# Adding the last two parts of a sum in SBUF instead of the last one

## The chip, the core and the metric

The kernel runs on one core of one Trainium2 chip. The metric is the device time of one execution, in microseconds (us). Before the change three runs took 773.85, 774.66 and 778.57 us, a median of 774.66 us.

## The reference

Attention in which a query sees only the keys of its own hash bucket, then two feed-forward layers, all in fp32. Cut to what matters here:

```
x = attention(q, k, v)                       # 2 x 8 heads, 768 tokens, 64 wide -> 1536 x 512
h = x @ w_in;  x = (h - tanh(h)) @ w_out     # first layer, hidden width 2048
g = x @ w_gate                               # second layer, hidden width 1536
out = (silu(g) * (x @ w_val)) @ w_out2       # 1536 x 512, fp32
```

The change lies in the last product, `... @ w_out2`.

## The kernel before

**Tiling.** The second layer goes over its hidden width in `NP2` = 6 parts of 256 columns, `i` = 0 to 5. Each part is computed for two halves of the tokens (`sb` = 0, 1, 768 tokens each) and each half for two blocks of 384 tokens (`t` = 0, 1). So there are four output blocks, called 0/0, 0/1, 1/0 and 1/1 here (`sb`/`t`), each 384 x 512. In each part a block has three output groups, `m` = 0 to 2, of 128 rows each: six matmuls (128 x 512, line 1099) into one PSUM bank. The products with `w_gate` and `w_val` (line 1045) come before the output groups of their part and are mixed with those of the part before, so that TensorE always has work.

**Where the sum over the parts is kept.** It lies in the output in HBM. Parts 0 to 4 copy each group out of PSUM into a stage in SBUF (line 1128, on ScalarE or VectorE). When the three groups of a block are there, one DMA of 768 KB carries them out: a plain store for part 0 (line 1143), and for parts 1 to 4 an accumulating DMA that GpSimd issues (line 1145), which adds the stage to the output. The stages are a ring of four, one for each block, in the tiles `acc_2601` (`sb` = 0) and `acc_2602` (`sb` = 1). Part 5 goes the other way: SyncE loads the block's sum from the output into its stage (line 1120), VectorE adds each group to it from PSUM (line 1123), and SyncE stores each group's 128 rows (line 1124). A load waits until the accumulating DMA of its block has landed, since both touch the same bytes of the output.

**PSUM.** An output group takes the next of four banks (`t`, `t`, `x`, `h`) and gives it back when its copy or its add has run.

**The order of the work.** Every operation of the program has a number, and `ORDER` lists for each engine the numbers in the order in which the engine runs them. Each engine is a queue: an instruction that waits holds up all behind it. SyncE runs the loads of the weights (line 461), of the sums and the last stores in one such queue, and GpSimd runs its arithmetic and the accumulating DMAs in another.

The last twelve output groups on TensorE are those of part 5, in the order 0/0, 0/1, 1/0, 1/1, three groups each.

Of the kernel before, what the change touches and what calls it, by code (L numbers as in the profile page):

```python
# [18 lines left out]
NB, NH, S, D = 2, 8, 768, 64  # L19
# [8 lines left out]
NP1, NP2 = F1 // 256, F2 // 256  # L28
# [18 lines left out]
def chunk_keys():  # L47
# [5 lines left out]
    for i in range(NP2):  # L53
# [51 lines left out]
    """,  # L105
    DVE="""
# [49 lines left out]
    """,  # L156
    ACT="""
# [40 lines left out]
    """,  # L198
    POOL="""
# [17 lines left out]
    """,  # L217
    SP="""
# [11 lines left out]
    """,  # L230
).items()}

# [1 line left out]
class Plan:  # L234
# [15 lines left out]
    def op(self, eng, fn, r=(), w=(), due=0.0, lat=None, late=False, after=0.0, alt=None, port=()):  # L250
        n = len(self.ops)
        deps = set()
        for k in r:
            deps.update(self.writers.get(k, ()))
        for k in w:
            deps.update(self.writers.get(k, ()))
            deps.update(self.readers.get(k, ()))
        for k in r:
            self.readers.setdefault(k, []).append(n)
        for k in w:  # L260
            if k in r:
                self.writers.setdefault(k, []).append(n)
            else:
                self.writers[k] = [n]
                self.readers[k] = []
        deps.discard(n)
        self.banks[n] = {k[:2] for k in (*r, *w) if k[0] == "s"}
        eng = {e: t * (1 if e == "PE" or not self.n_first else self.SAFE) for e, t in eng.items()}
        self.ops.append((eng, fn, deps, due, self.LAT if lat is None else lat, late, after,
                         ALT if alt is None else alt, port, self.PE_WAIT if "PE" in eng else 0.0))  # L270
# [100 lines left out]
def lsh_attention_moe_kernel(ctx: ExitStack, tc: tile.TileContext, qT, kT, vP, proj, cst, wts, out):  # L371
# [3 lines left out]
    op = plan.op  # L375
# [576 lines left out]
    stages = {}  # L952
# [124 lines left out]
    def out_group(layer, i, sb, j):  # L1077
# [6 lines left out]
        t, m = divmod(j, n)  # L1084
# [5 lines left out]
        def mm(e):  # L1090
# [12 lines left out]
           due=d, lat=0.25)  # L1103
        e = clock[0]
        aks = [("acc", sb, n * t + c) for c in range(n)]
        if layer == 1 and i in (0, NP1 - 1):
# [4 lines left out]
            else:  # L1111
                op({"DVE": dve(TB)}, lambda g: g.tensor_tensor(
                    out=acc_at(sb, j), in0=ps(), in1=acc_at(sb, j), op=ALU.add,
                ), r=[k, ("acc", sb, j)], w=[("acc", sb, j)], due=e, late=True)
        elif layer == 2 and i == NP2 - 1:
            if m == 0:
                parts = [stage(layer, c) for c in range(n)]
                stages["last"] = [(at_, key) for at_, key, _ in parts]
                o = out[sb * S + t * TB:sb * S + t * TB + TB, :].rearrange("(j p) c -> p j c", p=128)
                op({"SP": 0.5}, lambda g, at_=parts[0][0]: g.dma_start(out=at_(3).rearrange("p (j c) -> p j c", j=3), in_=o),  # L1120
                   r=[("o", sb, t)], w=[key for _, key, _ in parts] + [k for _, _, f in parts for k in f], due=e - 25, lat=4.0)
            at_, key = stages["last"][m]
            op({"DVE": dve(DM)}, lambda g: g.tensor_tensor(out=at_(), in0=ps(), in1=at_(), op=ALU.add), r=[k, key], w=[key], due=e)
            op({"SP": 0.5}, lambda g: g.dma_start(out=out[sb * S + j * 128:sb * S + j * 128 + 128, :], in_=at_()), r=[key], w=[], due=e)
        else:
            at_, key, first = stage(layer, m)
            op({"ACT": act(size), "DVE": dve(size)}, lambda g, at_=at_:
# [171 lines left out]
```

## Time and profile before

| what | value |
|---|---|
| median of 3 runs | 774.66 us (773.85 to 778.57) |
| the profiled execution | 775.52 us, its span 773.2 us |
| TensorE busy | 757.5 us, 98% of the span |
| VectorE busy | 602.1 us, 78% |
| ScalarE busy | 456.2 us, 59% |
| GpSimd busy | 359.8 us, 47% |

The span is what the trace covers; the execution's own time has 2.3 us around it. TensorE is the engine that is nearly always busy, so time can be saved only where it stands idle or runs at a lower clock, and lost wherever it is made to wait. [...]

### The profile page before, as it was taken

How to read it: one execution, taken by the hardware profiler on the slowest of the kernel's cores; microseconds unless marked ns; L12 is line 12 of the kernel's file. 1: busy time of each engine (PE TensorE's matmuls, PEld its weight loads, DVE VectorE, ACT ScalarE, POOL GpSimd, SP SyncE). 2: the span in 40 equal slices, each digit the busy share in tenths (PEclk: the TensorE clock that was granted, in tenths of full speed). 3: DMA queues.
4: the chain of work that ended last, by engine and by line, in shares of the span. 5: the costliest groups of instructions: out<-in, count | busy, mean ns of one | idle time of the engine just before them, and what ended most of it. 6: DMA issues, size and time to landing. Idle time of an engine off the chain costs nothing.

```text
span 773.2 us, 12380 instructions
## 1 busy us (share of the span) xinstructions
PE 757.5 (98%) x4342; PEld 666.8 (86%) x4342; DVE 602.1 (78%) x1075; ACT 456.2 (59%) x964; POOL 359.8 (47%) x387
## 2 busy tenths in 40 slices
PE   7999999999999999999999999999999999999996
PEld 4677677677767999999999999999999998999995
DVE  6878777888998678888677889998887768788373
ACT  5887788879876646555455456665554445545320
POOL 4755666966884743223124353734324544323120
PEclk9999999999999999999999999999999999999998
DMA  5754466356323016787585764323547476486486
GB/s 140 200 143 110 118 179 146 82 136 173 114 83 109 28 37 176 166 190 196 115 198 114 202 136 106 84 96 109 182 119 156 117 163 137 111 150 91 73 177 231
DMA packets 38733, 104.23 MB, mean 135 GB/s; under 512 B 4720, under 2 KB 10096, under 8 KB 38672
## 3 DMA queue, kind: packets, MB, share of 16 engines
q1 hardware_dynamic: 28288, 71.06, 29.9%
q0 software_dynamic: 9920, 31.59, 23.8%
q10 hardware_dynamic: 464, 0.80, 0.4%
q8 instruction: 34, 0.56, 0.3%
q14 instruction: 27, 0.22, 0.1%
HBM read 49.17 MB, written 18.87 MB: 88 GB/s over the span
## 4 chain that ended last, share of the span: by engine, by line
PE 87%; ACT 3%; DMA 3%; DVE 3%; POOL 2%; issue 1%; SPq 1%; ACTq 0%; DVEq 0%; POOLq 0%
PE bs L1045 31%; PE t L1099 16%; PE h L1099 7%; PE x L889 7%; PE s L836 7%; PE t L866 6%; PE x L1099 5%; PE x L1045 3%; ACT ct L848 2%; PE t L1045 2%; DVE m L846 1%; DMA acc<-out 1%; PE h L1045 1%; SPq L746 1%; POOL ct L855 1%
## 5 line engine op out<-in xcount | busy, mean ns | idle before, releaser
L1045 PE MATMUL bs<-x,wi 128*128 128x384 f32 x1200 | 231.4, 335 | 1.0 <-DVE ct L1028 1.0
L1045 PEld LDWEIGHTS bs<-x,wi 128*128 128x128 f32 x1200 | 210.6, 188 | 6.2 <-DVE ct L1028 1.7
L855 POOL TENSOR_SCALAR ct<-ct,r 128x768 f32<-128x768 f32 x96 | 94.2, 986 | 36.2 <-DVE r L854 23.9
L846 DVE TENSOR_REDUCE m<-s 128x1 f32<-128x768 f32 x96 | 91.0, 953 | 20.9 <-PE s L836 18.7
L848 ACT ACTIVATE ct<-s,m 128x768 f32<-128x768 f32 x96 | 86.5, 902 | 18.9 <-DVE m L846 8.3
L1025 ACT ACTIVATE ct<-bs 128x384 f32<-128x384 f32 x120 | 57.2, 490 | 67.6 <-PE bs L1045 63.2
L836 PE MATMUL s<-op 128*128 128x384 f32 x384 | 91.5, 362 | 2.7 <-ACT ct L848 2.3
L866 PE MATMUL t<-csb,ct 128*128 128x128 f32 x576 | 82.6, 275 | 2.1 <-ACT pt L872 1.0
L866 PEld LDWEIGHTS t<-csb,ct 128*128 128x128 f32 x576 | 66.8, 140 | 18.7 <-issue 5.6
L836 PEld LDWEIGHTS s<-op 128*128 128x128 f32 x384 | 63.8, 189 | 17.4 <-ACT ct L848 8.5
L872 ACT ACTIVATE pt<-t 128x384 f32<-128x384 f32 x135 | 62.2, 489 | 24.3 <-PE t L866 23.3
L1099 PE MATMUL t<-op,wo 128*128 128x384 f32 x384 | 75.7, 335 | 0.0
L889 PE MATMUL x<-pt,v 128*64 128x384 f32 x384 | 69.0, 494 | 0.0
L1099 PEld LDWEIGHTS t<-op,wo 128*128 128x128 f32 x384 | 67.2, 188 | 0.6 <-DVE ct L1128 0.3
L1099 PE MATMUL t<-wo,op 128*128 128x512 f32 x264 | 67.7, 393 | 0.0
L477 POOL TENSOR_TENSOR wi<-fs,wi 128x512 fp32r<-128x512 f32 (+1 forms) x29 | 45.5, 1569 | 38.9 <-ACT wi L475 38.1
L1136 POOL DMA_DIRECT2D acc<-ct x24 | 21.0, 888 | 78.5 <-ACT ct L1128 32.2
L1099 PEld LDWEIGHTS t<-wo,op 128*128 128x128 f32 x264 | 48.9, 188 | 8.3 <-DVE acc L1128 0.3
L889 PEld LDWEIGHTS x<-pt,v 128*64 128x64 f32 x384 | 24.7, 136 | 28.6 <-issue 28.0
L475 ACT ACTIVATE wi<-fs 128x512 fp32r<-128x512 f32 (+1 forms) x60 | 41.9, 701 | 12.2 <-DVE fs L495 3.8
L1145 POOL DMA_DIRECT2D out<-acc x16 | 20.8, 1300 | 57.5 <-ACT op L967 16.8
L1045 PE MATMUL bs<-op,wi 128*128 128x384 f32 x240 | 47.3, 334 | 0.0
(171 smaller groups left out, 1412.5 us busy)
## 6 DMA issues: line engine op xcount, KB each, us to landing
raw<-in_w SPq DMA_DIRECT2D x68, 512.0 KB, 3.5
acc<-ct POOLq DMA_DIRECT2D x24, 768.0 KB, 6.1
out<-acc POOLq DMA_DIRECT2D x16, 768.0 KB, 7.5
op<-raw SPq DMA_DIRECT2D x42, 192.0 KB, 3.2
op<-f SPq DMA_DIRECT2D x56, 96.0 KB, 3.3
v<-in_v SPq DMA_DIRECT2D x8, 384.0 KB, 4.2
out<-acc SPq DMA_DIRECT2D x4, 768.0 KB, 4.6
acc<-out SPq DMA_DIRECT2D x4, 768.0 KB, 5.8
```

What stands on the lines that cost most here:

```text
L475: op({"ACT": act(n)}, lambda e: e.activation(out=hi, in_=src, func=ACTF.Copy), r=rk, w=[wk + (0,)], due=due, late=late)
L477: op({"POOL": pool(n), "DVE": dve(n)}, lambda e: e.tensor_tensor(out=lo, in0=src, in1=hi.bitcast(F32), op=ALU.subtract), r=rk + [wk + (0,) ...
L836: g.matmul(out=s[:, kh, 0:TB], lhsT=(b, a)[first][:, q0], rhs=ks[kh][0 if first else 1], start=first, stop=not first,)
L846: op({"DVE": 0.87}, lambda g: g.tensor_reduce(out=m, in_=sv, axis=AX.XY, op=ALU.max, negate=True), r=[sk + (0,), sk + (1,)], w=[mk])
L848: op({"ACT": 0.9}, lambda g: g.activation(out=p.rearrange("p (a b) -> p a b", a=2), in_=sv, func=ACTF.Exp, bias=m, accum_out=sm), r=[sk + ...
L855: op({"POOL": 0.91}, lambda g: g.tensor_scalar(out=p, in0=p, scalar1=r, scalar2=1.0, op0=ALU.mult, op1=ALU.mult), r=[pk, rk], w=[pk])
L866: g.transpose(out=t_t[z][:, kt * 128:(kt + 1) * 128], in_=p[:, z * TB + kt * 128:z * TB + (kt + 1) * 128], identity=ident)
L872: g.activation(out=dst, in_=src, func=ACTF.Copy) if g is nc.scalar else g.tensor_copy(dst, src),
L889: g.matmul(out=x[r, :], lhsT=v[:, kt, r], rhs=pt_t[ptks[e][1]][:, kt, :], start=(kt == 0), stop=(kt == NKT - 1), tile_position=(0, 64 * e),)
L1025: op({"ACT": act(TB)}, lambda e: e.activation(out=dst, in_=bank(), func=ACTF.Copy), r=[bk], w=dk, due=due)
L1045: e.matmul(out=bank(), lhsT=w[:, wpart, wi * 256 + k * 128:wi * 256 + k * 128 + 128], rhs=x_at(sb, xn, xpart, k), start=first and m == 0, ...
L1099: e.matmul(out=ps(), lhsT=lhs, rhs=rhs, start=c == 0, stop=c == 5)
```

## The change

Part 4 now goes the way of part 5: at its first group the block's sum over parts 0 to 3 is loaded into the stage, and the groups of part 4 and then of part 5 are added there by VectorE. Only after part 5 are the rows stored. So the four loads stand one part earlier, the four accumulating DMAs of part 4 are gone, and twelve copies out of PSUM have become adds. The number of matmuls, of loads and of stores is the same. The lists of `ORDER` are written anew for the second layer, from its part 1 on; here two of the lines of SyncE's list stand for them.

```
@@ SyncE's list
-        3005 3077 3081 3153 3159 3167 3171 3243 3247 3319 3325 3356 3332 3334 3350 3358 3342 3376 3366 3361 3364
+        3005 3077 3081 3153 3159 3168 3172 3244 3248 3319 3166 3325 3214 3242 3288 3333 3349 3356 3341 3359 3362
...
@@ out_group
-        elif layer == 2 and i == NP2 - 1:
-            if m == 0:
+        elif layer == 2 and i >= NP2 - 2:
+
+            if m == 0 and i == NP2 - 2:
                 parts = [stage(layer, c) for c in range(n)]
-                stages["last"] = [(at_, key) for at_, key, _ in parts]
+                stages["last", sb, t] = [(at_, key) for at_, key, _ in parts]
...
-            at_, key = stages["last"][m]
+            at_, key = stages["last", sb, t][m]
             op({"DVE": dve(DM)}, lambda g: g.tensor_tensor(out=at_(), in0=ps(), in1=at_(), op=ALU.add), r=[k, key], w=[key], due=e)
-            op({"SP": 0.5}, lambda g: g.dma_start(out=out[sb * S + j * 128:sb * S + j * 128 + 128, :], in_=at_()), r=[key], w=[], due=e)
+            if i == NP2 - 1:
+                op({"SP": 0.5}, lambda g: g.dma_start(out=out[sb * S + j * 128:sb * S + j * 128 + 128, :], in_=at_()), r=[key], w=[], due=e)
```

In the rows of the order, `acc_2601` holds the stages of `sb` = 0 and `acc_2602` those of `sb` = 1; `out_0` is the output in HBM; a row without a count is one instruction. The changed file's list is one line shorter, so lines up to about 1110 have a number lower by one, and those behind the change one that is higher by one.

The end of SyncE's queue before: weights (line 461), loads of the sum (line 1120), stores (line 1124).

```order
L461 DMA raw_67<-in_w 128x512 x15
L1120 DMA acc_2601<-out_0 128x3x512 x2
L1124 DMA out_0<-acc_2601 128x512 x4
L1120 DMA acc_2602<-out_0 128x3x512 x2
L1124 DMA out_0<-acc_2601 128x512 x2
L1124 DMA out_0<-acc_2602 128x512 x6
```

The same place now (weights line 460, loads line 1120, stores line 1125):

```order
L460 DMA raw_67<-in_w 128x512 x12
L1120 DMA acc_2601<-out_0 128x3x512
L460 DMA raw_67<-in_w 128x512
L1120 DMA acc_2601<-out_0 128x3x512
L1120 DMA acc_2602<-out_0 128x3x512 x2
L1125 DMA out_0<-acc_2601 128x512 x6
L1125 DMA out_0<-acc_2602 128x512 x6
```

The two loads of `sb` = 1 stood behind four stores; now all four loads stand ahead of the first store, and one weight load has a load of the sum ahead of it.

The end of GpSimd's queue before: the accumulating DMAs (line 1145), the splits of weights (lines 477, 514) and of activations (line 962).

```order
L1145 DMA out_0<-acc_2601 128x3x512
L962 TENSOR_TENSOR op_86<-ct_90,op_86 128x384
L1145 DMA out_0<-acc_2602 128x3x512
...
L1145 DMA out_0<-acc_2602 128x3x512
L477 TENSOR_TENSOR wi_63<-fs_71,wi_63 128x768
L1145 DMA out_0<-acc_2602 128x3x512
L514 TENSOR_TENSOR wo_82<-f_75,wo_82 128x512
L1145 DMA out_0<-acc_2601 128x3x512
...
L1145 DMA out_0<-acc_2602 128x3x512 x2
```

And now (accumulating DMAs line 1146, splits lines 476, 513, 961):

```order
L1146 DMA out_0<-acc_2602 128x3x512
L513 TENSOR_TENSOR wo_80<-f_75,wo_80 128x512
...
L1146 DMA out_0<-acc_2601 128x3x512
L961 TENSOR_TENSOR op_86<-ct_90,op_86 128x384
L1146 DMA out_0<-acc_2602 128x3x512
...
L1146 DMA out_0<-acc_2602 128x3x512
L476 TENSOR_TENSOR wi_63<-fs_71,wi_63 128x768
L1146 DMA out_0<-acc_2602 128x3x512
L513 TENSOR_TENSOR wo_82<-f_75,wo_82 128x512
```

Of the last nine accumulating DMAs before, the last four (part 4) are gone. The five ahead of them keep their order: 0/0 of part 3, 1/1 of part 2, then 0/1, 1/0 and 1/1 of part 3. The one ahead of these five, 1/0 of part 2, had seven instructions between itself and them and has four now.

VectorE's queue before, near the end of part 4: copies (line 1128) among the arithmetic of part 5's activations.

```order
L1128 COPY acc_2602<-h_103 128x512
L962 TENSOR_TENSOR ct_90<-bs00_2406,ct_90 128x384
L1128 COPY acc_2602<-t_107 128x512
L1128 COPY acc_2602<-t_108 128x512
L962 TENSOR_TENSOR bs11_2396<-bs11_2396,ct_90 128x384
```

And now:

```order
L1123 TENSOR_TENSOR acc_2602<-h_103,acc_2602 128x512
L961 TENSOR_TENSOR ct_90<-bs00_2406,ct_90 128x384
L1123 TENSOR_TENSOR acc_2602<-t_107,acc_2602 128x512
L1123 TENSOR_TENSOR acc_2602<-t_108,acc_2602 128x512
L961 TENSOR_TENSOR bs11_2396<-bs11_2396,ct_90 128x384
```

The adds stand where copies stood. Over the whole program VectorE has 12 adds more (24 instead of 12), 2 copies fewer, and 6 fewer small instructions of the preparation, which are now GpSimd's; ScalarE has 10 copies fewer.

## Rows read from the trace of the kernel before

**Rows 1.** The page's busy time: us, share of the span, instructions.

```profile
PE 757.5 (98%) x4342; PEld 666.8 (86%) x4342; DVE 602.1 (78%) x1075; ACT 456.2 (59%) x964; POOL 359.8 (47%) x387
```

**Rows 2.** Waits of TensorE from 500 us on: total us, times, longest.

```profile
PE x L1099 <- DVE acc L1123: 2.7, 1, 2.7
PE bs L1045 <- DVE ct L1028: 1.0, 1, 1.0
```

**Rows 3.** The chain that ended last, its end: start us, us, what.

```profile
756.42 7.46 DMA acc<-out
...
763.97 0.70 DVE acc L1123
...
764.72 2.63 PE x L1099 x6
767.34 2.00 PE h L1099 x6
...
769.37 0.69 DVE acc L1123
```

**Rows 4.** The end by window: busy us by engine, granted clock, DMA share, GB/s.

```profile
762.00:765.00 3.00, 0.35 (x2) 0.29 (x2) 1.03 (x2) 0.00 (x0) 0.00 (x0) 1.00 0.76 294
765.00:767.00 2.00, 2.00 (x6) 1.58 (x6) 1.45 (x3) 0.00 (x0) 0.00 (x0) 0.52 0.76 281
767.00:769.50 2.50, 2.33 (x7) 1.46 (x6) 0.82 (x2) 0.00 (x0) 0.00 (x0) 0.70 0.75 280
```

**Rows 5.** TensorE's timeline: start us, us, line, what.

```profile
698.96 1.55 PE L1099 MATMUL t<-wo,op 128*128 128x512 f32 x6
...
710.66 1.55 PE L1099 MATMUL t<-wo,op 128*128 128x512 f32 x6
712.05 1.21 PE L1045 MATMUL bs<-op,wi 128*128 128x384 f32 x6
...
759.18 2.88 PE L1099 MATMUL t<-wo,op 128*128 128x512 f32 x12
```

**Rows 6.** What SyncE's queue waited for from 690 us on.

```profile
SPq L1120 <- DMA out<-acc: 49.2, 2, 38.2
```

**Rows 7.** SyncE's timeline: start us, us, line, what.

```profile
755.86 0.97 SPq L1120 DMA_DIRECT2D acc<-out  x2
```

**Rows 8.** DMA issues: queue, count, KB each, median us to landing.

```profile
out<-acc POOLq DMA_DIRECT2D x16, 768.0 KB, 7.5
...
acc<-out SPq DMA_DIRECT2D x4, 768.0 KB, 5.8
out<-acc SPq DMA_DIRECT2D x12, 256.0 KB, 2.2
```

**Rows 9.** GpSimd's timeline, part 3's accumulating DMAs: start us, us, idle before.

```profile
671.23 1.27 POOL L1145 DMA_DIRECT2D out<-acc  x1
...
688.50 1.29 POOL L1145 DMA_DIRECT2D out<-acc  x1 [7.36 <-ACT ct L1025]
...
696.80 1.30 POOL L1145 DMA_DIRECT2D out<-acc  x1 [5.96 <-ACT op L967]
...
704.29 1.30 POOL L1145 DMA_DIRECT2D out<-acc  x1 [4.30 <-DVE bs L1028]
```

**Rows 10.** Copies and adds out of PSUM: ns min/median/max, first and last start.

```profile
L1128 ACT ACTIVATE acc<-t x5: 599/599/600, 700.5 to 728.2; 128x512 f32<-128x512 f32 x5
L1128 DVE COPY acc<-t x3: 681/681/691, 716.8 to 739.8; 128x512 f32<-128x512 f32 x3
...
L1123 DVE TENSOR_TENSOR acc<-t,acc x6: 679/691/692, 746.6 to 765.8; 128x512 f32<-128x512 f32 x6
```

**Rows 11.** Part 4's stretch by window: busy us of PE, PEld, DVE, ACT, POOL.

```profile
680.00:700.00 20.00, 20.00 (x106) 18.51 (x105) 17.84 (x29) 10.95 (x22) 6.66 (x6) 1.00 0.76 135
700.00:720.00 20.00, 20.00 (x105) 18.33 (x104) 14.77 (x23) 8.33 (x17) 3.92 (x3) 1.00 0.71 113
720.00:740.00 20.00, 20.00 (x104) 18.38 (x103) 6.53 (x13) 7.10 (x15) 4.00 (x4) 1.00 0.48 103
```

75 rows, old and new, of tables (ACT, DVE, PE, POOL) are left out of this document.

## The prediction

> **What bounds the kernel now.** The page's busy times come first: TensorE is busy 757.5 us of a span of 773.2 us, and no other engine comes near it [rows 1]. With the same matmuls before and after, time can come only from TensorE's waits and from a clock below the full one. So the next view is TensorE's waits. From 500 us on, which holds all that the change touches, there are two: 1.0 us somewhere in the second layer, and 2.7 us for a VectorE add of line 1123 [rows 2]. The chain of waits tells where the second comes from. A load of the sum lands 7.46 us after its issue; the add behind it runs at 763.97; only then is a bank free for the group that starts at 764.72 [rows 3]. The last two groups then take 2.63 and 2.00 us, although a group takes 1.39 us elsewhere: the one at 710.66 gives way to the next work at 712.05 [rows 5]. [...]
>
> Why the load is late stands in SyncE's queue. The loads wait for the accumulating DMAs of part 4, 49.2 us in all [rows 6], and the second pair, for `sb` = 1, stands behind four stores (the order) and is issued from 755.86 on [rows 7], when TensorE needs the sums within a few microseconds.
>
> **The tail, which the change takes away.** In the changed order all four loads stand ahead of the first store and belong to part 4, so no group of part 5 waits for a DMA. Without the wait the last two groups follow the twelve matmuls that start at 759.18, which are two groups: 759.18 + 2 x 1.39 = 761.96, not 764.72. That is 2.76 us. At full clock the two take 2.78 us, not 2.63 + 2.00 = 4.63: 1.85 us more. Together **4.61 us**. What is late next? A group's bank is needed again three groups after the group ends, 3 x 1.39 = 4.17 us, and its add takes 0.69 us [rows 10], so the adds keep more than 3 us of room and the end stays one add and one store (2.2 us to landing [rows 8]) behind the last group, as now.
>
> **The loads, moved one part earlier.** They now wait for part 3's accumulating DMAs. In the trace those are issued at 671.23 (0/0), 688.50 (0/1), 696.80 (1/0) and 704.29 us (1/1) [rows 9]. The tightest of the pairs that I work out is 0/1: issued at 688.50, landed 7.5 us later [rows 8], at 696.0; a load as slow as the slowest seen, 7.46 us, ends at 703.5. TensorE is through with the first group of 0/1 at 712.05 [rows 5], and no add can run before. Room: 8.5 us. For 0/0 it is 671.23 + 7.5 + 7.46 = 686.2 against 698.96 + 1.39 = 700.35, 14.2 us. On SyncE one weight load now stands behind the first load and so behind an accumulating DMA that landed at 678.7; no row shows when TensorE would miss that weight, so I bound it by the same room and take nothing.
>
> GpSimd's queue decides those issue times. Two accumulating DMAs there stand 7.49 us apart, 696.80 and 704.29 [rows 9], which is one landing: the second seems to wait for the first. In the new order 1/0 of part 2 stands closer ahead of the five, so the chain may be pushed back, at worst by one landing of 7.5 us. That still fits into 8.5. Cost nothing; the cover is this room, and beyond it VectorE's queue would stand.
>
> **Copies into adds.** An add takes 0.691 us, a copy 0.681 on VectorE and 0.599 on ScalarE [rows 10]. Twelve adds more and two copies fewer on VectorE are 12 x 0.691 - 2 x 0.681 = 6.9 us; six small instructions leave it, so 6.9 is the upper end. It lies beside TensorE as long as VectorE has room: in part 4's stretch it is busy 17.84, 14.77 and 6.53 us of 20 [rows 11], so 2.2, 5.2 and 13.5 us are free. At least five copies there were ScalarE's [rows 10], 3.5 us more for VectorE, spread over 40 us. I take nothing; the other end is 6.9 us of waiting. ScalarE loses ten copies, 6.0 us, hidden as they were. GpSimd loses four issues of 1.3 us and the standing behind them, and gains some arithmetic: nothing on the path, since TensorE never waits for it here [rows 2]. Its four transfers of 768 KB go too; the matmuls wait for no transfer before the tail.
>
> **The lists anew.** The other wait, 1.0 us [rows 2], lies in the rewritten stretch. It may go, or a like one may come: between -1.0 and +1.0, I take 0.
>
> **Sum.** -4.61 us, all else 0. On the profiled execution: 775.52 - 4.6 = 770.9 us, a span of 768.6. The median of the three runs is 0.86 us below the profiled one: 774.66 - 4.6 = **770.1 us**. That is 0.6%, less than the 1% that a measurement here can tell from no change.
>
> **Rivals.**
>
> *The clock falls all the same.* Then only the idle time comes back: 774.66 - 2.76 = 771.9. For it: nothing shows that the two slow groups were slow for the gap alone. Against it: the clock is 1.00 in every part 4 window, where TensorE is always busy [rows 11], and is low only right behind the gap [rows 4]. [...] Here no row shows a low clock without a gap before it, so I give this 9%.
>
> *VectorE becomes the bound (slower).* The place is part 4: VectorE at 17.84 of 20 us before the stretch gets copies that were ScalarE's. If it falls behind, the banks come free late and TensorE stops. If all 6.9 us became waiting and the clock then cost 1.85 us as it did in the tail, 8.75 - 4.61 = 4.1 us is lost: 778.8. It decides from 2.8 us of waiting on, where 2.8 + 1.85 is the gain. For it: the first window's 89%. Against it: 21 us are free over the three windows, three times the addition. 7%.
>
> *A load of part 4 comes late.* The add at the head of VectorE's queue holds all its other work. It starts to count when a chain is over 8.5 us later than in the trace. Two landings more ahead of it, 15 us, leave 6.5 us of standing; the banks cover some 3.4 of it, so 3.1 + 1.85 us are lost against 4.61 won: 775.0. [...] 5%.
>
> **Chances and range.** The forecast has 77%, the rivals 9, 7 and 5%, and 2% is left for what none of them names. The forecast's own range is 770.1 less 1.0 (the other wait gone) and less 0.8 (the median against the lowest run, 773.85), and the same upward: 768.3 to 771.9. It takes in the clock rival just about. To leave out no more than 2 in 10 I reach partly into the slower cases: 768.3 to 773.6. Faster by over 1% (under 766.9) would take 7.8 us, more than the waits and the clock hold: 3%. Slower by over 1% (over 782.4) needs both slower cases at their worst: 4%. Within 1%: 93%.
>
> **What would show it.** In the profile after: no wait of TensorE for line 1123; the granted clock 1.00 up to its last group; the last six matmuls of 128 x 512 in about 1.4 us; four loads landed before 725 us, all ahead of the first store; twelve accumulating DMAs; TensorE's waits from 500 us on at 1 to 2 us in all. Wrong would be a wait of TensorE or VectorE between 680 and 745 us, on a load or on an add of part 4, or two slow groups at the end without a gap before them.

## The result, and the profile after

The changed kernel took 783.83 us (median of ten runs, 778.47 to 786.00), the kernel before in the same comparison 774.86 us (772.90 to 778.57). The ratio worked out from the runs is 1.0096, with a 95% interval of 1.0077 to 1.0115 (the two medians alone give 1.0116). So it is slower, by about 1%, where the forecast was 770.1 us and 0.6% faster. The profiled execution of the changed kernel is one of its quicker ones: 779.19 us, span 777.4, against 775.52 and 773.2 before. The traces below explain the 4.2 us between these two spans.

The page's busy time answers to [rows 1]: us, share of the span, instructions.

```profile
PE 757.4 (97%) x4342; PEld 667.9 (86%) x4342; DVE 601.2 (77%) x1079; ACT 451.0 (58%) x954; POOL 359.2 (46%) x389
```

TensorE is as busy as before. The time is in its waits. From 500 us on (total us, times, longest; answers to [rows 2]):

```profile
PE bs L1044 <- ACT ct L1024: 2.6, 1, 2.6
PE x L1044 <- DVE op L961: 2.1, 1, 2.1
PE bs L1044 <- DVE ct L1027: 2.1, 2, 1.4
```

TensorE's timeline says where they are (start us, us, line, what; in brackets the wait before):

```profile
608.47 3.28 PE L1044 MATMUL bs<-x,wi 128*128 128x384 f32 x12 [2.57 <-ACT ct L1024]
642.28 2.38 PE L1044 MATMUL bs<-x,wi 128*128 128x384 f32 x12 [0.70 <-DVE ct L1027]
669.77 1.31 PE L1044 MATMUL x<-x,wi 128*128 128x384 f32 x6 [2.14 <-DVE op L961]
693.87 2.35 PE L1044 MATMUL bs<-x,wi 128*128 128x384 f32 x12 [1.43 <-DVE ct L1027]
```

The wait for an add of line 1123 is gone, and four waits, 6.84 us together, stand where two, 1.02 and 2.65 us, stood. None is for a load of a sum. They are called the first to the fourth here; the second, 0.70 us, is for the same kind of instruction as the 1.02 us before, and the other three are new. The first and the third are also followed by a lower clock. The windows behind the first (busy us of PE, PEld, DVE, ACT, POOL, granted clock as a share of full speed, DMA share, GB/s):

```profile
609.00:610.00 1.00, 1.00 (x7) 1.00 (x6) 0.86 (x2) 1.00 (x3) 0.61 (x1) 0.80 0.72 295
610.00:611.00 1.00, 1.00 (x5) 1.00 (x4) 0.54 (x2) 0.73 (x2) 0.68 (x1) 0.50 0.00 0
...
612.00:613.00 1.00, 1.00 (x4) 0.81 (x3) 0.97 (x3) 0.73 (x2) 0.00 (x0) 0.50 0.00 0
```

What the clock withholds is the sum of (1 - clock) over the time: 0.2 + 3 x 0.5 = 1.7 us here, and the same again from 671 to 675 us (granted clock 0.52, 0.50, 0.50 and 0.77). At the end there is nothing of it. The end of the chain of waits answers to [rows 3]:

```profile
767.66 2.72 PE t L1098 x12
770.38 1.36 PE x L1098 x6
771.74 1.37 PE h L1098 x6
```

The groups follow each other without a gap and take 1.36 us, and the window there shows the full clock (answers to [rows 4]):

```profile
770.00:773.00 3.00, 3.00 (x14) 2.25 (x12) 1.38 (x2) 0.00 (x0) 0.00 (x0) 1.00 0.46 175
```

The account: waits 6.84 - 3.67 = +3.2 us, lower clock 2 x 1.7 - 1.7 = +1.7 us (before: 2 x 0.48 + 2.5 x 0.30 in [rows 4]), together +4.9 against +4.2 in the spans, 0.7 us too much. Most of that lies at the start: the same twelve matmuls (`x<-pt,v`) start at 86.10 us in the profile before and at 85.15 in this one, 0.95 us earlier.

**The first wait.** It goes back to SyncE, in part 0. In the kernel before, the last plain store of part 0, block 1/1, was issued at 573.31 us. Now it stands behind two more weight loads, and a weight load waits until VectorE has freed its buffer, here up to 14.8 us (`SPq L460 <- DVE fs L468`). SyncE's timeline:

```profile
560.81 0.43 SPq L1144 DMA_DIRECT2D out<-acc  x1
567.80 25.75 SPq L460 DMA_DIRECT2D raw<-in_w  x4
593.64 1.09 SPq L1144 DMA_DIRECT2D out<-acc  x1
```

The chain of waits continues from there:

```profile
593.64 8.10 DMA out<-acc
...
601.76 0.04 DVE acc L1129
...
604.32 2.11 DVE ct L961
...
608.03 0.39 ACT ct L1024
...
608.47 3.28 PE bs L1044 x12
```

The store reads its stage until 601.74, and the copy of the next part into that stage stands at the head of VectorE's queue until then, 2.79 us; ScalarE's copy waits 2.35 us. All of VectorE's work behind it is late. On top of that, one of its instructions on this chain (`ct<-ct`) now runs beside a split of weights on GpSimd and takes 2.19 us, where it takes 0.56 as a rule:

```profile
603.62 2.40 POOL L476 TENSOR_TENSOR wi<-fs,wi 128x768 fp32r<-128x768 f32 x1 [3.65 <-ACT wi L474]
604.24 2.19 DVE L961 TENSOR_TENSOR ct<-ct 128x384 f32<-128x384 f32 x1
```

So TensorE's wait comes from the late store and from a stretched instruction together; the experiment with the stores early shows how the two hang together.

**The third wait.** Here one instruction of VectorE takes 4.29 us. VectorE and GpSimd, start us, us, idle in brackets:

```profile
663.41 1.29 POOL L1146 DMA_DIRECT2D out<-acc  x1
...
664.24 1.79 POOL L513 TENSOR_TENSOR wo<-f,wo 128x512 fp32r<-128x512 f32 x1
664.50 4.29 DVE L465 SCALAR_TENSOR_TENSOR fs<-raw,fs 128x512 uint32<-128x512 uint32 x1
665.49 1.51 POOL L961 TENSOR_TENSOR ct<-ct 128x384 f32<-128x384 f32 x1
666.47 1.76 POOL L476 TENSOR_TENSOR wi<-fs,wi 128x512 fp32r<-128x512 f32 x1
...
669.18 0.54 DVE L961 TENSOR_TENSOR op<-x,op 128x384 fp32r<-128x384 f32 x1
```

The same instruction (ns min/median/max) takes 684 ns as a rule:

```profile
L465 DVE SCALAR_TENSOR_TENSOR fs<-raw,fs x40: 675/684/4291, 185.0 to 692.1; 128x512 uint32<-128x512 uint32 x40
```

It lasts until three splits on GpSimd, one behind the other, have run. Behind it in the queue is `op<-x,op`, for which TensorE waits 2.14 us. The accumulating DMA ahead of the splits is that of block 1/0 of part 2, at 649.36 us before and at 663.41 us now.

`raw` and `fs` are both in SBUF, and the 4.29 us end 0.56 us behind the third split, about the 0.68 us that the instruction takes alone: it looks as if it had stood until the splits were through and then run. What makes it stand is not shown, and the order of the starts does not settle it. Here VectorE's instruction starts 0.26 us behind the first split; at 704.49 us in the kernel before, and at 678.41 us in an experiment below, it starts over 0.6 us ahead of the split and is held all the same (2.97 and 2.72 us). GpSimd's times in a trace are rough, so this stays open.

**The fourth wait** has a cause of the same kind, at one remove:

```profile
683.28 1.51 POOL L961 TENSOR_TENSOR ct<-ct 128x384 f32<-128x384 f32 x1
683.37 1.71 DVE L462 TENSOR_SCALAR fs<-raw 128x512 uint32<-128x512 uint32 x1
...
687.25 0.33 SPq L460 DMA_DIRECT2D raw<-in_w  x1
687.75 0.38 SPq L1120 DMA_DIRECT2D acc<-out  x1
...
691.72 0.43 DVE L462 TENSOR_SCALAR f<-raw 128x512 uint32<-128x512 uint32 x1 [2.57 <-DMA raw<-in_w]
```

The instruction at 683.37 takes 1.71 us, where the like one at 688.73 takes 0.42. VectorE frees the weights' buffer late, the next weight load is issued late, and VectorE then waits for it. A load of the sum was issued 0.5 us behind that weight load, which made it a suspect as well.

### The profile page after: what moved, and what is told of

Read it like the earlier page. It is cut to its first block, busy times and chain, and to the rows that moved or that the text cites. A ratio compares the mean times of both kernels' runs of the same rounds, so it can differ in the third digit from the quotient of the medians.

```text
span 777.4 us, 12377 instructions
## 1 busy us (share of the span) xinstructions
PE 757.4 (97%) x4342; PEld 667.9 (86%) x4342; DVE 601.2 (77%) x1079; ACT 451.0 (58%) x954; POOL 359.2 (46%) x389
## 4 chain that ended last, share of the span: by engine, by line
PE 83%; DVE 6%; DMA 4%; ACT 2%; POOL 2%; issue 1%; SPq 0%; DVEq 0%; ACTq 0%; POOLq 0%
PE bs L1044 28%; PE t L1098 15%; PE x L888 8%; PE s L835 7%; PE h L1098 7%; PE t L865 6%; PE x L1098 5%; PE x L1044 2%; PE t L1044 2%; DMA raw<-in_w 1%; DVE m L845 1%; POOL ct L854 1%; ACT ct L847 1%; DMA out<-acc 1%; PE h L1044 1%
## 5 line engine op out<-in xcount | busy, mean ns | idle before, releaser
L961 POOL TENSOR_TENSOR ct<-ct 128x384 f32<-128x384 f32 x23 | 25.6, 1112 | 54.2 <-ACT ct L980 36.1
L961 POOL TENSOR_TENSOR op<-ct,op 128x384 fp32r<-128x384 f32 x31 | 34.7, 1153 | 32.4 <-ACT op L966 23.1
```

What stands on the lines that cost most here:

```text
L961: op({"DVE": dve(TB), "POOL": pool(TB)} if port else {"DVE": dve(TB) + 0.01}, lambda e: e.tensor_tensor(out=now(dst), in0=now(a), in1=b, o ...
```

## The experiments

The theory: the sum itself, changed as the diff says, gains what the forecast says, and the new lists lose more than that, by the late stores on SyncE and by GpSimd's splits beside VectorE. The rivals: the sum costs the time (its loads or its adds), or the clock does by itself. Numbers in the edits are operations: 2540 and 2624 are the stores of part 0 of blocks 0/1 and 1/1, 2949 is the accumulating DMA of 663.41, 3170 the instruction of 4.29 us, 2977 the one TensorE waits for, 3166 the first load of a sum, 3325 the last weight load. In the table "after" is the changed kernel; most rows are ten or twelve runs, the last one seven, and the old sum in the new lists and the load behind alone four. Each ratio is to runs of the kernel before made alongside (medians 775.13 to 775.73 us).

| kernel | median us | lowest to highest | ratio to before [95%] |
|---|---|---|---|
| changed sum, lists of before | 772.90 | 770.93 to 774.92 | 0.9962 [0.9938, 0.9986] |
| old sum, new lists | 786.53 | 784.99 to 788.65 | 1.0130 [1.0087, 1.0174] |
| after, stores early | 775.13 | 773.23 to 781.14 | 1.0007 [0.9976, 1.0037] |
| after, split behind | 779.31 | 774.87 to 783.11 | 1.0046 [1.0021, 1.0071] |
| after, both | 773.99 | 770.62 to 778.88 | 0.9984 [0.9963, 1.0006] |
| after, both and the load behind | 773.61 | 771.91 to 776.75 | 0.9977 [0.9962, 0.9991] |
| after, the load behind alone | 783.42 | 779.60 to 784.89 | 1.0096 [1.0068, 1.0124] |
| after, stores and the DMA early | 772.94 | 771.28 to 778.26 | 0.9976 [0.9954, 0.9999] |
| changed sum, lists of before, one split moved | 770.81 | 768.89 to 773.12 | 0.9936 [0.9913, 0.9960] |

### The changed sum in the lists of before

The adds take the places of the copies, and the four loads stand behind the last weight load:

```
@@ SyncE
-2578 2821 2827 2835 2540 2839 2911 2915 2987 2624 2993 ... 3319 3166 3325 3214 3242 3288
+2578 2821 2827 2540 2835 2839 2911 2624 2915 2987 2993 ... 3319 3325 3166 3214 3242 3288
@@ the other lists: those of before, with adds for copies
```

> The changed sum (parts 4 and 5 added in SBUF), but with the lists of before: ten instructions of ScalarE's and VectorE's copies of part 4 become VectorE's adds at the places where the copies ran, the four accumulating DMAs of part 4 leave GpSimd's list, and the four loads stand right behind the last weight load on SyncE. Theory 'lists' (the sum in SBUF gains the tail's 4.6 us, and the new lists lose 9 or more): about 774.9 - 4.6 = 770.3 us, no wait of TensorE for line 1123, no wait over 1.5 us between 560 and 740 us. Rival 'adds' (more work on VectorE and earlier loads make TensorE wait in parts 3 and 4, whatever the lists): 776 to 784 us, with waits of 2 us and more between 640 and 740 us.

Measured: 772.90 against 775.13 us, faster by 0.4%, and the rival's 776 to 784 us are ruled out. The end is free of its wait, as in the changed kernel. But not all of the 4.6 us came: a wait of 1.01 us near 714.7 us is new, which the last experiment takes up.

### The old sum in the new lists

```
-        elif layer == 2 and i >= NP2 - 2:
-            if m == 0 and i == NP2 - 2:
+        elif layer == 2 and i == NP2 - 1:
+            if m == 0:
@@ the end of each list: that of before; up to part 4 the new lists
```

> The sum as before (only part 5 added in SBUF), but with the new lists up to part 4 and the tail's order of before. Theory 'lists': it has both losses, the waits of the new lists and the tail's, so the changed kernel's 783.8 + 4.6 = about 788 us (783 to 790). Rival 'adds': about 775 us, as before, since the lists alone cost nothing.

Measured: 786.53 us. The waits near 611, 645, 672 and 697 us are there without any change to the sum (2.88, 1.69, 2.13 and 3.62 us), and the one at the end is back with 2.41 us. Over the kernel before, the new lists cost 11.4 us here; the sum is not the cause.

### The stores of part 0 early

```
@@ SyncE
-2578 2821 2827 2835 2540 2839 2911 2915 2987 2624 2993
+2578 2821 2827 2540 2835 2839 2911 2624 2915 2987 2993
```

> The changed kernel with one edit: on SyncE the stores of part 0 of blocks 0/1 and 1/1 go back to their places of before, ahead of one and of two weight loads. Theory 'late store': the wait of VectorE and ScalarE for that store (2.8 and 2.35 us at 601.8 us) goes, and with it TensorE's wait of 2.57 us at 605.9 and the half clock behind it (some 1.7 us): about 4.3 us faster than the changed kernel, 779.5 us. Rival 'port': VectorE is late there since its instructions stretch beside GpSimd's (2.19 in place of 0.55 us at 604.2), so TensorE waits 1.5 us or more near 606 all the same, and the time stays within 1.5 us of 783.8.

Measured: 775.13 us, 8.7 us under the changed kernel by the medians and 0.9% by the ratios, where 4.3 us (0.55%) were expected. In the trace the store is issued at 575.82 us, and the wait near 608 and the lower clock behind it are gone (granted clock 1.00 from 600 to 640 us), so the rival falls. The stretch that the rival names was brought about by the late store itself: now `ct<-ct` comes ahead of the split and takes its usual time.

```profile
602.78 0.55 DVE L961 TENSOR_TENSOR ct<-ct 128x384 f32<-128x384 f32 x1
...
604.63 1.85 POOL L476 TENSOR_TENSOR wi<-fs,wi 128x768 fp32r<-128x768 f32 x1 [3.23 <-ACT wi L474]
```

What the rest of the gain is, the one profile does not show: its execution took 777.72 us and still waits 2.14 and 2.78 us near 667 and 692. One hint is the clock. Four of the ten runs, 773.23 to 774.09 us, have a mean granted clock of 0.999 or 1.000, the ten of the changed kernel 0.989 to 0.995; a stretch that withholds 1.7 us lowers the mean by 0.002. So those four can't have had the lower clock behind the wait near 667 in full either.

### The stretched instruction behind the two that TensorE needs

```
@@ VectorE
-3170 3042 2977
+3042 2977 3170
```

> The changed kernel with one edit: on VectorE the weight instruction that took 4.29 in place of 0.68 us at 664.5 us, beside an accumulating DMA and three GpSimd instructions in a row, moves behind the two instructions that TensorE waits for. Theory 'port': TensorE's wait of 2.14 us at 667.6 goes, and the half clock behind it (some 1.7 us): 3.8 us faster than the changed kernel, about 780 us; the moved instruction still stretches if it meets GpSimd's. Rival 'too much work on VectorE': the wait only moves to the next instruction, the sum of TensorE's waits between 640 and 700 us stays at 3.5 to 4.5 us, and the time within 1 us.

Measured: 779.31 us, a ratio of 1.0046 where after has 1.0096, about as the theory says. The moved instruction still takes 2.17 us beside GpSimd, but the wait near 668 is gone, with its lower clock, and so is the one near 692; the first wait (2.9 us) stays, and one of 1.05 us near 716 is new. The profiled execution took 774.87 us, 4.4 under the median of the ten, so what the others wait for is not seen.

### Both

The two edits above together.

> The changed kernel with both edits at once: part 0's stores early on SyncE, and the stretched weight instruction behind the two that TensorE waits for on VectorE. Theory 'lists': the two losses are separate, so both waits (2.6 us near 606, 2.1 us near 668) and both stretches of half clock go; left is the wait near 692 us of 1.4 to 2.8 us for a weight load: about 772 us, 3 us under the first edit alone (775.1). Rival 'one cause' (both edits only move the same lateness): no less than the first edit alone, 775 us.

Measured: 773.99 us, between the two expectations. Waits of 1.23, 0.39, 0.20 and 0.96 us remain, and no lower clock shows behind any of them: the six matmuls of a group take 1.20 to 1.31 us (128x384) and 1.55 to 1.57 us (128x512) there, where they took up to 2.01 and 2.23 us behind the third and the first wait of the changed kernel. By the medians the edits gain 8.7 and 4.5 us alone and 9.8 together, so the two losses overlap and are not a plain sum.

### Both, and the first load of a sum behind the weights

```
@@ SyncE
-3319 3166 3325 3214
+3319 3325 3166 3214
```

> As the kernel with both edits, and the first load of the sum moves on SyncE behind the last weight load. Theory 'load beside weights': the weight load issued just ahead of that load lands in 3.5 in place of 4.5 to 6.0 us, VectorE does not wait for it near 690 us, TensorE's wait there (1.4 to 2.8 us) goes, and the loads of the sum still land in time: 770 to 771 us, about 1 to 2 us under the kernel with both edits. Rival: the weight load is slow because of the accumulating DMAs, so the wait stays and the time is the same within 0.5 us.

Measured: 773.61 us: the edit changes nothing that can be measured beside the two others, as the rival said. But the wait that it aims at was down to 0.39 us in the kernel with both edits, so there was little to gain; the next experiment is the real test.

### The load behind the weights alone

> The changed kernel with that one edit alone: the first load of the sum behind the last weight load on SyncE. Theory 'load beside weights': TensorE's wait of 1.43 us near 692 us goes, nothing else: 1.4 us under the changed kernel. Rival: the wait stays; within 0.5 us of the changed kernel.

Measured: 783.42 us, ratio 1.0096: a miss. The fourth wait is still there, as the rival said, and longer than in the first profile of the changed kernel (TensorE's timeline):

```profile
696.07 4.21 PE L1044 MATMUL bs<-x,wi 128*128 128x384 f32 x12 [2.80 <-DVE ct L1027]
```

So the load of the sum beside the weight load is not what makes the fourth wait.

### The changed kernel once more

> The changed kernel once more, for its trace: most of its runs took 783 to 786 us, while the profiled one took 779.2. Theory 'clock': a run near 784 us has the same waits of TensorE, and one or two stretches of half clock more (1.7 us each), behind the waits near 642 or 692 us; a run near 779 us has the two stretches seen. Rival: another wait, not seen so far.

Measured: 784.18 us, span 782.4, one run. Its waits are 3.16, 0.60, 2.14 and 3.17 us at 611.09, 644.79, 672.27 and 698.13; the lower clock lasts as long as in the first profile (it withholds 1.7 us behind the first and 1.7 us behind the third). So neither expectation holds: the waits are the same four, two of them longer, with no more of the lower clock. 2.2 of the 5.0 us to the first profile are waits. The first wait begins at 607.93 us, in the first profile at 605.90: another 2.0 us lie ahead of all that is discussed here. Nearly all of them are there before 90 us (the twelve matmuls `x<-pt,v` start at 87.06 in place of 85.15), far ahead of the part that the lists change; what they are is not shown. The rest of 0.8 lies mostly behind the last add, which starts 5.0 us before the end of the span here and 4.3 us before it there.

### The stores and the accumulating DMA early

The edit on the stores, and on GpSimd:

```
-3085 3086 3089 2972 3087 2984 2949 3164 3031 3093
+3085 3086 2949 3089 2972 3087 2984 3164 3031 3093
```

> The changed kernel with the two stores of part 0 early (775.1 us in its runs), and on GpSimd the accumulating DMA of part 2's block 1/0 four instructions earlier, about where it stood before. Theory (its late place pushes three splits together beside VectorE's weight instruction): the weight instruction takes at most 2.5 us in place of 4.29, TensorE's wait near 667 falls from 2.14 to under 0.6 and the lower clock behind it goes, as the wait near 692 does; 772 to 773.6 us. Rival (the three splits stand together by themselves, the DMA ahead of them is only a neighbour): the instruction stays above 3.5 us, both waits stay, 775.1 give or take 0.8.

Measured: 772.94 us, within the theory's range, though its ratio (0.9976) can't be told from that of the stores alone (1.0007): the intervals overlap. The stretched instruction and its neighbours:

```profile
660.57 1.29 POOL L513 TENSOR_TENSOR wo<-f,wo 128x512 fp32r<-128x512 f32 x1
...
661.64 0.77 DVE L465 SCALAR_TENSOR_TENSOR fs<-raw,fs 128x512 uint32<-128x512 uint32 x1
661.83 1.46 POOL L961 TENSOR_TENSOR ct<-ct 128x384 f32<-128x384 f32 x1
```

With the DMA gone from ahead of the splits, VectorE's instruction falls into the seam between two of them and takes 0.77 us; the wait of 2.14 us near 667 is gone. That part is as the theory says. The other part is not: this profiled execution, 777.06 us where the median of the twelve is 772.94, has a fourth wait of 3.85 us:

```profile
678.23 1.30 POOL L1146 DMA_DIRECT2D out<-acc  x1 [6.33 <-issue]
678.41 2.72 DVE L468 SCALAR_TENSOR_TENSOR fs<-raw,fs 128x512 uint32<-128x512 uint32 x1
679.06 1.52 POOL L961 TENSOR_TENSOR ct<-ct 128x384 f32<-128x384 f32 x1
...
681.16 0.33 SPq L460 DMA_DIRECT2D raw<-in_w  x1
...
687.12 0.62 DVE L462 TENSOR_SCALAR f<-raw 128x512 uint32<-128x512 uint32 x1 [4.06 <-DMA raw<-in_w]
...
689.45 2.95 PE L1044 MATMUL bs<-x,wi 128*128 128x384 f32 x10 [3.85 <-DVE ct L1027]
```

The third and the fourth wait are thus separate: each goes back to a split on GpSimd that meets a VectorE instruction with its inputs in SBUF (4.29 us long in the changed kernel, 2.72 us here). In the kernel with both first edits the same weight load came at 679.80, because VectorE's instruction ahead of it (679.10) ran in 0.68 us, 1.81 us before that accumulating DMA; the fourth wait was 0.39 us. The DMA's start hangs on the landing of the one before (in the trace of the changed kernel four in a row, from 682.44 to 708.91 us, start 0.32 us after it), so the meeting can differ from run to run. That this makes the spread of the runs is likely, but it was only argued.

### The changed sum in the lists of before, one split moved to VectorE

In that kernel, the wait near 714.7 us followed from this (its timeline):

```profile
708.95 1.29 POOL L1146 DMA_DIRECT2D out<-acc  x1 [6.40 <-DVE op L961]
...
709.78 1.78 POOL L513 TENSOR_TENSOR wo<-f,wo 128x512 fp32r<-128x512 f32 x1
...
710.01 1.98 DVE L961 TENSOR_TENSOR ct<-ct 128x384 f32<-128x384 f32 x1
```

```
@@ GpSimd
-3115 3256 3146 3330 3229
+3115 3256 3146 3229
@@ VectorE
-3210 3215 3219
+3210 3215 3330 3219
```

> The changed sum in the lists of before (772.9 us in its runs), with one weight split (line 513, wo) taken from GpSimd and given to VectorE a few instructions later. Theory (GpSimd's arithmetic stretches VectorE's instructions that read SBUF twice): the activation split at 710 takes about 0.55 us in place of 1.98, TensorE's wait of 1.0 us near 714.7 goes, and the time is 771.9 (771.3 to 772.5). Rival (the issue of the accumulating DMA at 708.95 stretches it): it stays above 1.2 us, the wait stays, and the time is 772.9, half a microsecond either way.

Measured: 770.81 us, ratio 0.9936: the quickest of all kernels, 0.6% under the kernel before. The instruction beside the same DMA now:

```profile
707.12 1.29 POOL L1146 DMA_DIRECT2D out<-acc  x1 [6.37 <-DVE op L961]
...
708.20 0.56 DVE L961 TENSOR_TENSOR ct<-ct 128x384 f32<-128x384 f32 x1
```

It starts 0.21 us before the DMA's issue has ended, as it did then (0.23 us), and takes 0.56 us: the arithmetic split did the stretching and not that issue. The trace of the kernel before bears this out: `wi<-fs,wi` at 595.87 us lies wholly inside such an issue (595.84 to 597.14), with no split beside it, and takes its usual 0.68 us. TensorE is left with one wait of 1.42 us from 500 us on. The gain is larger than the 1.0 us of the wait, but the intervals of the two ratios overlap.

## Why the prediction was wrong

**The step that failed is "The lists anew": "between -1.0 and +1.0, I take 0".** It bounded a whole rewritten stretch by the one wait that stood there. The old sum in the new lists measures that term: +11.4 us. Two mechanisms make it up: a plain store of part 0 behind two more weight loads, and GpSimd's splits beside VectorE's instructions. Undone together, with the changed sum left as it is, the time falls from 783.83 to 773.99 us, 9.8 of the 10.9 us to the same sum in the lists of before (772.90); the 1.1 us left are within the noise, as the intervals of the two ratios overlap. The first of the two works in part through the second: the late store brings `ct<-ct` beside a split. Neither was among the rivals, and the 2% left for the unnamed was far too little for lists written anew from part 1 on.

Both could have been asked before. The prediction named the place of the second mechanism, "1/0 of part 2 stands closer ahead of the five", but followed only the chain of landings from it, not what the moved DMA does to the splits behind it. Such stretches were in the trace of before too: 15 instructions of VectorE from 500 us on ran beside a split on GpSimd over 0.25 us longer than the median of their kind, 15.1 us in all, the longest at 704.49:

```profile
704.49 2.97 DVE L477 TENSOR_TENSOR wi<-fs,wi 128x512 fp32r<-128x512 f32 x1
```

TensorE waited for none of these for long. In the changed kernel there are fewer, 11 with 11.7 us, and they cost more: it is the place that counts. "Nothing on the path, since TensorE never waits for it here" was wrong of GpSimd for this reason; it reaches TensorE through VectorE (4.29 us of an instruction, 2.14 us of TensorE's wait). Both mechanisms begin ahead of the stretch the prediction looked at, 680 to 745 us.

**The tail** was right: no wait, full clock, the last groups in 1.36 us, worth 4.61 us by [rows 3 to 5]; before, TensorE's granted clock was 0.55 from 765 to 766 us and 0.50 from 766 to 768, behind the wait of 2.65 us. Its part for the clock, 1.85 us, is not lost in every execution, though: in the old sum in the new lists the last two groups took 1.66 and 1.37 us behind a wait of 2.41 us. **The clock rival** fell with it: in the traces before and after, the granted clock is below 1.00 only behind waits of TensorE (2.65 us before, 2.57 and 2.14 us now) and where TensorE has no work left.

**The loads one part earlier** were right: the last is issued before 719.1 us, and VectorE's adds wait for TensorE alone, 10.1 us in 15 waits, most of them in this row of VectorE's waits from 690 us on (us, times, longest):

```profile
DVE acc L1123 <- PE t L1098: 7.3, 10, 2.2
```

The weight load behind the first of them, taken at nothing, costs nothing: moving it gave 783.42 and 773.61 us, where the kernels without the move have 783.83 and 773.99. Part 3's accumulating DMAs start at 674.89, 689.87, 699.48 and 708.91 us, 1.4 to 4.6 us later than in [rows 9]; that stays within the room of 8.5.

**Copies into adds** were nearly right. In the lists of before the changed sum gains 2.2 us on the medians in place of 4.6, and 1.0 of the difference is the wait near 714.7, again a split beside VectorE; the other 1.4 us are not traced. VectorE did not become the bound: in the changed kernel its window of 680 to 700 us (answers to [rows 11]) is less busy than before, since it waits, and in the lists of before it is busy 16.89, 17.50 and 7.55 us in the three windows, 2.8 us more in all, while TensorE loses only the 1.0 us. The window in the changed kernel:

```profile
680.00:700.00 20.00, 18.57 (x98) 16.99 (x97) 15.33 (x27) 9.79 (x21) 5.16 (x5) 1.00 0.87 187
```

With that last split moved, the changed sum measures 770.81 us, next to the 770.1 that the sum of the prediction gave. The prediction took 0.6% to be too little to tell from no change; this kernel's interval, 0.9913 to 0.9960, does tell it.

## What to carry to other kernels

A gain that is worked out from one wait holds only if the rest of the order stays; where lists are written anew, compare them engine by engine over the whole rewritten stretch, and price each store and each DMA that moves past another. An engine for which TensorE never waits can still stretch the instructions of the one it does wait for, as here from 0.68 to 4.29 us. The way to part the two effects is two kernels: the new computation in the old order, and the old computation in the new order.

## What the runs showed of the hardware

A VectorE instruction with two inputs in SBUF took 4.29 us in place of 0.68 beside three GpSimd splits, and 0.77 us when it fell into the seam between two. In the traces before and after, from 500 us on, the 81 and 79 VectorE instructions that read PSUM and ran beside a split took at most 0.02 us more than the median of their kind (the adds of line 1123 took at most 0.69 us); the 15 and 11 that were stretched by over 0.25 us read SBUF alone.

From 500 us on, the granted clock fell to 0.50 behind waits of 2.14 us and more (2.65 us before; 2.57 and 2.14 us in the changed kernel), and behind none up to 1.94 us, but not behind every longer one: in the kernel with the load alone moved, the waits of 2.74 us (to 611.02) and 2.14 us were followed by the full clock, and that of 2.80 us (to 696.07) by the lower one (windows, columns as above):

```profile
611.00:614.00 3.00, 2.98 (x16) 2.84 (x17) 2.07 (x5) 2.29 (x5) 1.30 (x1) 1.00 0.37 150
...
695.00:698.00 3.00, 1.93 (x6) 1.93 (x7) 2.96 (x6) 1.29 (x3) 1.00 (x1) 0.56 0.90 158
```
